# A gated layer computed by Strassen's scheme: product M6 ahead of M5 in the quads without a tile after M6, and five smaller moves

## The chip, the cores and the metric

The kernel runs on one core of one Trainium2 chip. The metric is the device time of one execution in microseconds (us), smaller is better. The times of the kernel before are 2017.08, 2018.61 and 2018.64 us, median 2018.61.

## What is computed

Three layers follow one another on 2304 tokens of 512 features. Attention over pooled keys and a mixture of eight experts come first; the change touches neither. The third layer is the one changed:

```python
g = x @ w_gate                           # 2304x512 by 512x1536
silu = g * (1.0 / (1.0 + np.exp(-g)))
val = x @ w_val
return (silu * val @ w_out).astype(np.float32)
```

## The kernel before

**Numbers.** Every fp32 product is made of three matmuls: both operands are split into a high and a low part, and high*high, high*low and low*high are summed in PSUM (`mm3`, L117 to L119).

**Quads.** Tokens go in three passes of 768. A matrix product of a token block with 256 columns of weights is done by Strassen's scheme: seven half-size products M1 to M7 of six matmuls each instead of eight. One such group is a *quad* (`quad`, L1130). M1, M6, M7 and M4 are summed one after the other in PSUM bank a (`aps`), M2 goes to bank b (`bps`), M5 and M3 to bank c (`cps`). The order written out is M1, M2, M5, M6, M7, M4, M3. After M1, M6 and M7 ScalarE copies the state of bank a to SBUF (`part_sum`, L1113: copies s1, u2, u3); the next product into bank a has to wait for that copy. VectorE then adds the copies to banks b and c (`whole`, L1199), which gives the four quarters "11", "22", "21", "12".

**Gate and value.** The gated layer takes a gate quad and a value quad in turn for each 256 of the 1536 columns (loop variable `m`, six per pass). A gate quad ends each quarter with a sigmoid on ScalarE (L1606) and a product on VectorE (L1607). A value quad multiplies its quarters by them (L1622 in pass 1, L1636 in passes 2 and 3). In pass 1 the result is split (L1626, L1627) and the second layer follows as six plain token tiles (`yps`, L1184 to L1186, added on VectorE at L1788), which `fill_y` puts after M6 and after M7 of the next two quads. In passes 2 and 3 the second layer is by Strassen too, over two values of `m`, so over four quads (x = 0 gate, 1 value, 2 gate, 3 value): `split_b` (L1355 to L1357), the sums `sum_t13` and `sum_t24` (L1361, L1365), the splits `split_t` (L1346 on ScalarE, L1348 on GpSimd), and seven *blocks* (`gated_block`, `mbs`, L1684 to L1686, 18 matmuls each), put after M7 of x = 0 and after M2 and M7 of x = 1, 2, 3. No block and no tile stands after M6. VectorE adds each block to SBUF (L1691). When a pass is complete, `finish` (L1666) adds the blocks to the output rows (L1659) and stores them.

**What sets the order.** The program's order on each engine is written by hand: each quad takes a table `tasks` of work to issue after each of its products, and a queue `late` of work that is issued one step later. An engine works strictly in that order. So the sigmoid of "11" (issued late, after M5) stands ahead of the copy u2 in ScalarE's queue.

**Weights of the output matrix.** In pass 1 each gate quad also prepares 256 rows of `w_out` for the later passes: two row splits (L65, L66), four row sums on VectorE (`take_row_sums`, L190), their split (`split_gated_sums`, L879 on ScalarE, L882 on GpSimd), and stores to DRAM (`store_rows`, `store_gated_sums`, L886). The split sets return in passes 2 and 3 through three slots of 512 KB (`gated_set`, `load_gated`, L1652).

Of the kernel before, what the change touches and what calls it, by code (L numbers as in the profile page):

```python
# [29 lines left out]
def fused_kernel(ctx: ExitStack, tc, q, k, v, w_gate, w1, w2, v_gate, v_val, v_out, out):  # L30
# [8 lines left out]
    P = 128  # L39
# [576 lines left out]
    with tc.manual_schedule():  # L616
# [173 lines left out]
        def load_rows(i):  # L790
            if i < NQ or NE <= i < NE + NG:
                if i < NE + 2:
# [77 lines left out]
        def gated_row_sums(i):  # L870
            for f in take_row_sums(nc.vector, rraw[i], part_of(10.5, 8 * P, F32).rearrange("p (m f) -> p m f", m=4)):
                f()
# [259 lines left out]
        def quad(i, ys, tasks, sink, back=0):  # L1132
# [28 lines left out]
            prod(c, "M5", True)  # L1161
            after("M5")
# [3 lines left out]
            fill_y(per - back)  # L1166
# [3 lines left out]
            fill_y(per)  # L1170
# [47 lines left out]
        def next_weights(i, n, tasks, first=False):  # L1218
# [13 lines left out]
            if n is not None:  # L1232
# [14 lines left out]
                if not expert:  # L1247
                    at("M5", lambda: gated_row_sums(n))
                    at("M4", split_gated_sums)
# [395 lines left out]

        def gated_set(v):
            return part_of(60.5 + 4 * (v % 3), 8 * P).rearrange("p (q h f) -> p q h f", q=2, h=2)
# [27 lines left out]
        def gated_block(v, at_once=False):  # L1675
# [11 lines left out]
            load_gated(v + 3)  # L1687
# [15 lines left out]
        def pair_tasks(m, x, tasks):  # L1703
# [11 lines left out]
            if x == 0 and j:  # L1715
                merge(tasks, {"M6": [lambda: split_t(1, "M6", "22", G)], "M4": [lambda: split_t(1, "M5", "11", G)]})
            if j == 0 and x == 3:
# [4 lines left out]
        for m in range(NPASS * SP2):  # L1722
# [9 lines left out]
            if m < 2:  # L1732
                if m:
                    merge(tasks, {"M1": [lambda: split_rows(NE, 0), lambda: split_rows(NE, 1)],
                                  "M2": [lambda: store_rows(NE), lambda: gated_row_sums(NE)],
                                  "M5": [lambda: load_rows(NE + 1)], "M4": [split_gated_sums]})
# [12 lines left out]
            quad(i, more, tasks, gate_sink(gs, m, g), 2 if m == 1 else 0)  # L1749
# [21 lines left out]
            quad(i + 1, more, tasks, pair_sink(gs, g) if p else value_sink(gs, hs, n))  # L1771
# [63 lines left out]
```

## Time and profile before

| what | value |
|---|---|
| device time, three runs | 2017.08, 2018.61, 2018.64 us |
| the profiled execution | 2015.87 us |
| its span, first to last instruction | 2014.0 us |
| TensorE (PE) busy | 1965.8 us, 98% |
| VectorE (DVE) busy | 1494.9 us, 74% |
| GpSimd (POOL) busy | 1391.4 us, 69% |
| ScalarE (ACT) busy | 909.8 us, 45% |
| mean granted TensorE clock | 0.998 |
| the gated layer in the span | about 1575 to 2014 us |
| its pass 1, pass 2, pass 3, the end | to 1700, to 1838, to 1988, to 2014 |

Busy times say which engine has the least room. PE has, so what can be gained is its idle time: the waits of PE, stretch by stretch, and the work on another engine that ends each of them. A matmul of 384 columns is listed with 0.34 us, but the next one starts 0.17 us after it, so products are measured from start to start.

### The profile page before, as it was taken

Reading aid. Unit: us, or ns where it says so; the run is one execution under the profiler, and the core shown is the slowest. Engines: PE = TensorE matmul, PEld = TensorE weight load, DVE = VectorE, ACT = ScalarE, POOL = GpSimd, SP = SyncE. Lnnn points to the kernel's source line nnn. Section 1 sums busy time; section 2 is a strip of 40 time slices with the busy share of each in tenths; the row PEclk is TensorE's granted clock in tenths of the full one; section 3 lists DMA queues with packets and bytes.
Section 4 is the critical chain, followed back from the end, with each engine's and each line's share of the span. In section 5 each row is a group of like instructions: output and inputs, shape, how many; then the busy total and the mean of one; then the engine's idle time right before and its main releaser. Section 6 shows DMA issues by size and latency. Waiting matters only on the chain.

```text
span 2014.0 us, 32218 instructions
## 1 busy us (share of the span) xinstructions
PE 1965.8 (98%) x11405; PEld 1881.1 (93%) x11405; DVE 1494.9 (74%) x2310; ACT 909.8 (45%) x1751; POOL 1391.4 (69%) x1260
## 2 busy tenths in 40 slices
PE   8999999999999999999999999999999999998998
PEld 7899899899999999999999999999999888898997
DVE  7764868777777778777877888777777877667766
ACT  4443434444444534443434434444445555555552
POOL 7674668887888367767677667776776777676554
PEclk9999999999999999999999999999999999999999
DMA  7674587888888898889898898899886664644544
GB/s 201 188 197 126 216 286 252 320 304 312 291 316 303 302 327 320 317 302 317 298 324 310 280 334 318 306 310 317 310 302 237 226 244 152 214 158 157 188 161 142
DMA packets 230223, 528.03 MB, mean 262 GB/s; under 512 B 36176, under 2 KB 116144, under 8 KB 226224
## 3 DMA queue, kind: packets, MB, share of 16 engines
q1 hardware_dynamic: 226896, 522.85, 75.1%
q0 software_dynamic: 3168, 3.15, 1.1%
q8 instruction: 90, 1.47, 0.3%
q14 instruction: 69, 0.57, 0.1%
HBM read 370.16 MB, written 155.76 MB: 261 GB/s over the span
## 4 chain that ended last, share of the span: by engine, by line
PE 88%; DVE 7%; ACT 2%; issue 2%; DMA 1%; POOL 0%; SPq 0%; DVEq 0%; ACTq 0%; POOLq 0%
PE aps L117 8%; PE aps L119 8%; PE aps L118 8%; PE mbs L117 7%; PE mbs L118 7%; PE mbs L119 7%; PE yps L1184 4%; PE yps L1186 4%; PE yps L1185 4%; PE cps L117 4%; PE cps L119 4%; PE cps L118 4%; PE bps L117 2%; PE bps L118 2%; PE bps L119 2%
## 5 line engine op out<-in xcount | busy, mean ns | idle before, releaser
L1348 POOL TENSOR_TENSOR LR<-LF,LR 128x384 fp32r<-128x384 f32 x288 | 314.7, 1116 | 185.1 <-ACT LR L1346 184.9
L1113 ACT COPY LF<-aps 128x384 f32<-128x384 f32 x378 | 181.6, 480 | 407.9 <-PE aps L119 406.1
L117 PE MATMUL mbs<-LR 128*128 128x384 f32 x840 | 283.1, 337 | 0.0
L118 PE MATMUL mbs<-LR 128*128 128x384 f32 x840 | 282.5, 336 | 0.0
L119 PE MATMUL mbs<-LR 128*128 128x384 f32 x840 | 281.9, 336 | 0.0
L1395 DVE TENSOR_TENSOR AC<-mbs,AC 128x768 f32<-128x768 f32 x196 | 187.1, 955 | 126.6 <-PE mbs L119 126.1
L851 POOL TENSOR_TENSOR LR<-praw,LR 128x512 fp32r<-128x512 f32 (+1 forms) x130 | 136.9, 1074 | 106.0 <-ACT LR L843 105.9
L851 POOL TENSOR_TENSOR LR<-sums,LR 128x512 fp32r<-128x512 f32 (+1 forms) x101 | 168.0, 1678 | 23.9 <-ACT LR L843 23.9
L1184 PE MATMUL yps<-LR 128*128 128x512 f32 x432 | 169.5, 392 | 0.5 <-DVE AC L1447 0.5
L1361 POOL TENSOR_TENSOR LF<-LF 128x384 f32<-128x384 f32 x120 | 129.8, 1082 | 57.2 <-DVE LF L1515 45.4
L1186 PE MATMUL yps<-LR 128*128 128x512 f32 x432 | 168.7, 391 | 0.0
L1185 PE MATMUL yps<-LR 128*128 128x512 f32 x432 | 168.3, 390 | 0.0
L1355 ACT COPY LF<-bps 128x384 f32<-128x384 f32 x144 | 69.3, 481 | 217.3 <-DVE bps L1515 183.7
L118 PEld LDWEIGHTS mbs<-LR 128*128 128x128 f32 x840 | 157.8, 188 | 0.0
L119 PEld LDWEIGHTS mbs<-LR 128*128 128x128 f32 x840 | 157.7, 188 | 0.0
L117 PEld LDWEIGHTS mbs<-LR 128*128 128x128 f32 x840 | 157.6, 188 | 0.0
L1346 ACT ACTIVATE LR<-LF 128x768 fp32r<-128x768 f32 x144 | 122.0, 848 | 48.9 <-PE mbs L119 43.2
L1449 DVE SCALAR_TENSOR_TENSOR AC<-yps,pr,AC 128x512 f32<-128x512 f32 x168 | 121.2, 744 | 30.8 <-PE yps L1186 27.0
L1365 POOL TENSOR_TENSOR LF<-LF 128x384 f32<-128x384 f32 x120 | 132.3, 1103 | 9.4
L1199 DVE TENSOR_TENSOR bps<-cps,LF 128x384 f32<-128x384 f32 x126 | 70.8, 562 | 74.8 <-ACT LF L1113 74.5
L66 POOL TENSOR_TENSOR LR<-LF,LR 128x1024 fp32r<-128x1024 f32 x24 | 60.3, 2512 | 69.2 <-ACT LR L65 63.9
L66 POOL TENSOR_TENSOR LR<-rraw,LR 128x512 fp32r<-128x512 f32 x64 | 88.5, 1405 | 28.3 <-ACT LR L65 23.9
(341 smaller groups left out, 6228.3 us busy)
## 6 DMA issues: line engine op xcount, KB each, us to landing
LR<-w1s_d SPq DMA_DIRECT2D x210, 512.0 KB
LR<-w2s_d SPq DMA_DIRECT2D x210, 512.0 KB
w1s_d<-LR SPq DMA_DIRECT2D x29, 1792.0 KB
w2s_d<-LR SPq DMA_DIRECT2D x24, 1024.0 KB
w2s_d<-LR SPq DMA_DIRECT2D x90, 256.0 KB
LR<-w3s_d SPq DMA_DIRECT2D x42, 512.0 KB
praw<-in_moe_w_dram SPq DMA_DIRECT2D x30, 512.0 KB
rraw<-in_moe_w_dram SPq DMA_DIRECT2D x30, 512.0 KB
```

The lines of the kernel that those rows point to most:

```text
L66: nc.gpsimd.tensor_tensor(out=lo, in0=src, in1=hi.bitcast(F32), op=ALU.subtract)
L117: nc.tensor.matmul(ps, lhsT=wh, rhs=ah, start=start, stop=False, skip_group_check=more)
L118: nc.tensor.matmul(ps, lhsT=wh, rhs=al, start=False, stop=False, skip_group_check=more)
L119: nc.tensor.matmul(ps, lhsT=wl, rhs=ah, start=False, stop=stop, skip_group_check=more)
L851: nc.gpsimd.tensor_tensor(out=lo[:, c], in0=src[:, c], in1=hi[:, c].bitcast(F32), op=ALU.subtract)
L1113: nc.scalar.copy(out=t, in_=ps[:, :HB])
L1184: nc.tensor.matmul(ps, lhsT=hh[:, o:o + P], rhs=wh, start=j == 0, stop=False)
L1185: nc.tensor.matmul(ps, lhsT=hh[:, o:o + P], rhs=wl, start=False, stop=False)
L1186: nc.tensor.matmul(ps, lhsT=hl[:, o:o + P], rhs=wh, start=False, stop=j == 1)
L1348: eng.tensor_tensor(out=lo[:, c], in0=src[:, c], in1=hi[:, c].bitcast(F32), op=ALU.subtract)
L1365: eng.tensor_tensor(out=r_of(q, a), in0=r_of(q, a), in1=r_of(q, b), op=ALU.subtract)
L1395: nc.vector.tensor_tensor(out=acc_of(m), in0=ps[:, :, :HB], in1=acc_of(m), op=ALU.add)
```

## The change

1. `quad` gets an argument `swap`: the order is then M1, M2, M6, M5, M7, M4, M3. It is set in all quads of passes 2 and 3 and in the gate quad of m = 1. Tiles that stood after M6 go after M7.
2. The four row sums L190, which were issued together after M5, are issued two after M4 and two after M3 of the gate quad (m = 1: of both quads). Their split moves into the value quad, after M1, and the store after M7. The raw rows of one `w_out` part get a place of their own.
3. At the start of pass 3 the sums `sum_t13` and `sum_t24` of the pass before are issued after M4 and M3 of x = 0 instead of M1 and M2, the splits after them in x = 1.
4. `finish` issues its seven additions in other places.
5. At the end, the first of the last seven blocks is issued between the two sums.
6. Three of the last four weight sets go to another, free region and are loaded in the last quad, the fourth when the first of the last seven blocks is done.

```diff
-        def quad(i, ys, tasks, sink, back=0):
+        def quad(i, ys, tasks, sink, back=0, swap=False):
...
             c = new_c()
-            prod(c, "M5", True)
-            after("M5")
+            if not swap:
+                prod(c, "M5", True)
+                after("M5")
             prod(a, "M6", False)
             u2 = part_sum(a, "u2")
             after("M6")
-            fill_y(per - back)
+            if swap:
+                prod(c, "M5", True)
+                after("M5")
+            else:
+                fill_y(per - back)
             prod(a, "M7", False)
             u3 = part_sum(a, "u3")
             after("M7", ("22", c, u3))
-            fill_y(per)
+            fill_y(len(ys) - back if swap else per)
...
         def gated_row_sums(i):
-            for f in take_row_sums(nc.vector, rraw[i], part_of(10.5, 8 * P, F32).rearrange("p (m f) -> p m f", m=4)):
-                f()
+            t = part_of(10.5, 8 * P, F32).rearrange("p (m f) -> p m f", m=4)
+            steps = deque()
+
+            def two():
+                if not steps:
+                    steps.extend(take_row_sums(nc.vector, rraw[i], t))
+                for _ in range(2):
+                    steps.popleft()()
+
+            return {"M4": [two], "M3": [two]}
...
         def finish(p, m, other):
             V = nc.vector
-            return {"M1": [add_of(V, "M2", "M1"), add_of(V, "M6", "M1")],
-                    "M2": [out_rows(p, "M2", 0, 0)],
-                    "M6": [add_of(V, "M7", "M6"), add_of(other, "M3", "M6")],
-                    "M5": [add_of(other, "M3", "M5"), out_rows(p, "M3", 0, 1)],
+            return {"M2": [add_of(V, "M2", "M1"), out_rows(p, "M2", 0, 0)],
+                    "M6": [add_of(V, "M6", "M1"), add_of(other, "M3", "M6")],
+                    "M5": [add_of(V, "M7", "M6"), add_of(other, "M3", "M5"), out_rows(p, "M3", 0, 1)],
...
+            change = j > 0 and j % NGP == 0
             if x in (0, 2) and (x or j):
                 q = 0 if x else 1
-                merge(tasks, {"M1": [lambda: sum_t13(q, V)], "M2": [lambda: sum_t24(q, V)]})
+                m1, m2 = ("M4", "M3") if change and x == 0 else ("M1", "M2")
+                merge(tasks, {m1: [lambda: sum_t13(q, V)], m2: [lambda: sum_t24(q, V)]})
...
+            if x == 3 and 7 * (j + 1) == len(GORDER):
+                merge(tasks, {"M1": [lambda v=v: load_gated(v) for v in range(LAST, LAST + 3)]})
...
                 if m == 2:
-                    merge(tasks, {"M1": [lambda: store_gated_sums(NE + 1)]})
+                    merge(tasks, {"M5": [split_gated_sums], "M7": [lambda: store_gated_sums(NE + 1)]})
+                merge(tasks, gated_row_sums(n))
...
             elif 1 < m < SP2:
-                merge(tasks, {"M5": [lambda: store_gated_sums(n)]})
+                merge(tasks, {"M1": [split_gated_sums], "M7": [lambda: store_gated_sums(n)]})
...
+        while side:
+            side.popleft()()
+        v = len(GORDER) - 7
         sum_t13(1, nc.vector)
+        gated_block(v, True)
         sum_t24(1, nc.vector)
         split_t(1, "M6", "22", nc.gpsimd)
         split_t(1, "M5", "11", nc.gpsimd)
-        while side:
-            side.popleft()()
-        for k in range(7):
-            gated_block(len(GORDER) - 7 + k, True)
+        for k in range(1, 7):
+            gated_block(v + k, True)
```

Line numbers grow by 10 to 30 in the changed kernel. The pieces below show what stands on two engines' queues, first before, then after the change.

ScalarE at x = 0 of a regular pair in pass 2: a split L1346 of the quad ahead (L1358 after the change), copies of bank a (L1113; L1123), the sigmoid of "11" (L1606 from bank b; L1618), the weight split (L843; L845).

```order
L1346 ACTIVATE LR<-LF 128x2x384
L1113 COPY LF<-aps 128x384
L1606 ACTIVATE LF<-bps 128x384
L1113 COPY LF<-aps 128x384
L843 ACTIVATE LR<-praw_17380 128x2x256
L843 ACTIVATE LR<-praw_17380 128x256
```

```order
L1358 ACTIVATE LR<-LF 128x2x384
L1123 COPY LF<-aps 128x384 x2
L1618 ACTIVATE LF<-bps 128x384
L845 ACTIVATE LR<-praw_17379 128x2x256
L845 ACTIVATE LR<-praw_17379 128x256
```

The copies s1 and u2 now follow each other, and the sigmoid of "11" stands behind u2.

VectorE from the gate quad of m = 2 into its value quad: the sigmoid products (L1607; L1619), tile additions (L1788; L1812), additions of a copy to a bank (L1199; L1214), the row sums (L190 in both), the value products (L1622; L1634).

```order
L190 TENSOR_TENSOR LF<-AC 128x256
L190 TENSOR_TENSOR LF<-AC,LF 128x256
L1607 TENSOR_TENSOR LF<-bps,LF 128x384
L1788 TENSOR_TENSOR AC<-yps,AC 128x512 x2
L1199 TENSOR_TENSOR bps<-cps,LF 128x384
L1788 TENSOR_TENSOR AC<-yps,AC 128x512
L1607 TENSOR_TENSOR LF<-bps,LF 128x384
L1607 TENSOR_TENSOR LF<-aps,LF 128x384
L1199 TENSOR_TENSOR cps<-cps,LF 128x384
L1607 TENSOR_TENSOR LF<-cps,LF 128x384
L1199 TENSOR_TENSOR bps<-bps,LF 128x384
L1622 TENSOR_TENSOR bps<-bps,LF 128x384
```

```order
L1214 TENSOR_TENSOR bps<-cps,LF 128x384
L1812 TENSOR_TENSOR AC<-yps,AC 128x512
L1619 TENSOR_TENSOR LF<-bps,LF 128x384
L190 TENSOR_TENSOR LF<-AC 128x256
L190 TENSOR_TENSOR LF<-LF,AC 128x256
L1619 TENSOR_TENSOR LF<-aps,LF 128x384
L1214 TENSOR_TENSOR cps<-cps,LF 128x384
L190 TENSOR_TENSOR LF<-AC 128x256
L190 TENSOR_TENSOR LF<-AC,LF 128x256
L1619 TENSOR_TENSOR LF<-cps,LF 128x384
L1214 TENSOR_TENSOR bps<-bps,LF 128x384
L1634 TENSOR_TENSOR bps<-bps,LF 128x384
```

Before, all four sums (two of them are the first rows of the piece) stand ahead of the addition for "22" (bps<-cps); after, two stand ahead of the addition for "12" (cps<-cps) and two ahead of the one for the next quad's "11" (bps<-bps).

VectorE at the end of the program: sums `sum_t13` and `sum_t24` (L1361, L1365; L1373, L1377), the blocks' additions (L1691; L1708), the additions of `finish` (L1659; L1674).

```order
L1361 TENSOR_TENSOR LF<-LF 128x384 x2
L1365 TENSOR_TENSOR LF<-LF 128x384 x2
L1691 TENSOR_TENSOR AC<-mbs,AC 128x768
L1659 TENSOR_TENSOR AC<-AC 128x768 x2
L1691 TENSOR_TENSOR AC<-mbs,AC 128x768 x3
L1659 TENSOR_TENSOR AC<-AC 128x768
L1691 TENSOR_TENSOR AC<-mbs,AC 128x768 x2
L1659 TENSOR_TENSOR AC<-AC 128x768
L1691 TENSOR_TENSOR AC<-mbs,AC 128x768
```

```order
L1373 TENSOR_TENSOR LF<-LF 128x384 x2
L1708 TENSOR_TENSOR AC<-mbs,AC 128x768
L1377 TENSOR_TENSOR LF<-LF 128x384 x2
L1708 TENSOR_TENSOR AC<-mbs,AC 128x768 x2
L1674 TENSOR_TENSOR AC<-AC 128x768
L1708 TENSOR_TENSOR AC<-mbs,AC 128x768
L1674 TENSOR_TENSOR AC<-AC 128x768
L1708 TENSOR_TENSOR AC<-mbs,AC 128x768
L1674 TENSOR_TENSOR AC<-AC 128x768
L1708 TENSOR_TENSOR AC<-mbs,AC 128x768
L1674 TENSOR_TENSOR AC<-AC 128x768
L1708 TENSOR_TENSOR AC<-mbs,AC 128x768
```

The first block's addition now stands between the sums, and the two additions of `finish` behind it are gone from there.

## Rows read from the trace of the kernel before

**Rows 1.** the page, busy time, share of the span and instructions of each engine

```profile
PE 1965.8 (98%) x11405; PEld 1881.1 (93%) x11405; DVE 1494.9 (74%) x2310; ACT 909.8 (45%) x1751; POOL 1391.4 (69%) x1260
```

**Rows 2.** stretches: length, busy (count) PE PEld DVE ACT POOL, clock, DMA, GB/s

```profile
1838.00:1860.00 22.00, 17.65 (x100) 16.50 (x99) 19.34 (x27) 12.62 (x24) 16.99 (x13) 0.92 0.40 142
...
1988.00:2014.00 26.00, 17.91 (x131) 17.32 (x130) 17.00 (x20) 3.18 (x5) 16.91 (x11) 0.90 0.48 159
```

**Rows 3.** PE's waits (total, times, longest): 1575:1700, 1700:1743, 1743:1838, 1860:1988, 1988:2014

```profile
PE cps L117 <- DVE bps L1199: 4.9, 4, 2.1
PE aps L117 <- ACT LF L1113: 0.6, 1, 0.6
...
PE aps L117 <- ACT LF L1113: 2.1, 3, 0.8
PE cps L117 <- DVE bps L1199: 0.2, 1, 0.2
...
PE aps L117 <- ACT LF L1113: 5.5, 8, 1.2
...
PE aps L117 <- ACT LF L1113: 6.9, 11, 0.8
...
PE mbs L1684 <- DVE AC L1691: 1.9, 1, 1.9
PE mbs L1684 <- DMA LR<-w3s_d: 0.6, 1, 0.6
```

**Rows 4.** timeline, one quad of pass 2: start, us, engine, instruction, [idle <-releaser]

```profile
1757.39 0.34 PE L117 MATMUL cps<-T1h,LR 128*128 128x384 f32 x1
...
1758.43 0.34 PE L117 MATMUL aps<-T2h,LR 128*128 128x384 f32 x1
...
1759.30 0.34 PE L119 MATMUL aps<-T2h,LR 128*128 128x384 f32 x1
...
1759.67 0.48 ACT L1113 COPY LF<-aps 128x384 f32<-128x384 f32 x1 [1.76 <-PE aps L119]
...
1760.20 0.45 PE L117 MATMUL aps<-T3h,LR 128*128 128x384 f32 x1 [0.57 <-ACT LF L1113]
...
1761.36 0.28 PE L1684 MATMUL mbs<-LR 128*128 128x256 f32 x1
```

**Rows 5.** timeline, regular x = 0: copy s1, first matmul after M2

```profile
1792.05 0.48 ACT L1113 COPY LF<-aps 128x384 f32<-128x384 f32 x1
...
1792.58 0.34 PE L117 MATMUL cps<-T1h,LR 128*128 128x384 f32 x1
```

**Rows 6.** timeline, pass 2's first gate quad: the same two

```profile
1703.98 0.34 PE L117 MATMUL cps<-T1h,LR 128*128 128x384 f32 x1
...
1704.04 0.47 ACT L1113 COPY LF<-aps 128x384 f32<-128x384 f32 x1
```

**Rows 7.** timeline of pass 3's first gate quad, PE and ScalarE

```profile
1841.74 0.42 PE L117 MATMUL cps<-T1h,LR 128*128 128x384 f32 x1 [1.04 <-DVE LF L1636]
...
1842.18 0.50 ACT L1113 COPY LF<-aps 128x384 f32<-128x384 f32 x1
...
1846.24 0.49 ACT L1606 ACTIVATE LF<-bps 128x384 f32<-128x384 f32 x1 [2.82 <-DVE bps L1199]
...
1847.16 0.44 PE L117 MATMUL aps<-T3h,LR 128*128 128x384 f32 x1 [3.08 <-ACT LF L1113]
```

**Rows 8.** sums L190: whole kernel (ns min/median/max), stretch 1575:1700 (busy)

```profile
L190 DVE TENSOR_TENSOR LF<-rraw x52: 412/950/1512, 304.9 to 1601.3; 128x256 f32<-128x256 f32 x52
...
1575.00:1700.00 125.00, 31.04 (x24) 0.00 (x0) 1.00 0.64 219
```

**Rows 9.** timeline of the end, GpSimd and VectorE

```profile
1995.15 5.34 POOL L1348 TENSOR_TENSOR LR<-LF,LR 128x384 fp32r<-128x384 f32 x4 [2.02 <-ACT LR L1346]
...
2002.20 7.02 POOL L1659 TENSOR_TENSOR AC<-AC 128x768 f32<-128x768 f32 x3 [1.71 <-DVE AC L1691]
...
2008.49 0.96 DVE L1691 TENSOR_TENSOR AC<-mbs,AC 128x768 f32<-128x768 f32 x1 [0.96 <-PE mbs L1686]
```

More of the change, by code (lines that the diff above doesn't have):

```diff
@@ L791, in load_rows @@
             if i < NQ or NE <= i < NE + NG:
-                if i < NE + 2:
+                if i == NE + 1:
+                    rraw[i] = part_of(88.5, 8 * P).bitcast(F32).rearrange("p (j d) -> p j d", j=2)
+                elif i < NE + 1:
                     rraw[i] = rawp.tile([P, 2, DM], F32, tag="raw", name=f"rraw{i}")
@@ L1246, in next_weights @@
                 at("M3", lambda: store_rows(n))
-                if not expert:
-                    at("M5", lambda: gated_row_sums(n))
-                    at("M4", split_gated_sums)
             at("M5", lambda: pair_sums(i + 1))
@@ L1644, in fused_kernel @@
         GORDER = [(j, m) for j in range((NPASS - 1) * NGP) for m in GX]
+        LAST = len(GORDER) - 4
         def gated_set(v):
-            return part_of(60.5 + 4 * (v % 3), 8 * P).rearrange("p (q h f) -> p q h f", q=2, h=2)
+            at = 32.5 + 4 * (v - LAST) if LAST <= v < LAST + 3 else 60.5 + 4 * ((v - 6 if v > LAST else v) % 3)
+            return part_of(at, 8 * P).rearrange("p (q h f) -> p q h f", q=2, h=2)
         def load_gated(v):
@@ L1686, in gated_block @@
                     nc.tensor.matmul(y, lhsT=hl, rhs=w[:, q, 0], start=False, stop=q == 1)
-            load_gated(v + 3)
+            if v + 3 < LAST:
+                load_gated(v + 3)
+            elif v == LAST - 3:
+                load_gated(LAST + 3)
             if j % NGP == 0:
@@ L1709, in pair_tasks @@
             V, G = nc.vector, nc.gpsimd
+            change = j > 0 and j % NGP == 0
             if x in (0, 2) and (x or j):
                 q = 0 if x else 1
-                merge(tasks, {"M1": [lambda: sum_t13(q, V)], "M2": [lambda: sum_t24(q, V)]})
+                m1, m2 = ("M4", "M3") if change and x == 0 else ("M1", "M2")
+                merge(tasks, {m1: [lambda: sum_t13(q, V)], m2: [lambda: sum_t24(q, V)]})
             if x == 3:
                 merge(tasks, {"M4": [lambda: split_t(0, "M6", "22", G)], "M3": [lambda: split_t(0, "M5", "11", G)]})
-            if x == 0 and j:
+            if x == 1 and change:
+                merge(tasks, {"M2": [lambda: split_t(1, "M6", "22", G)], "M5": [lambda: split_t(1, "M5", "11", G)]})
+            if x == 0 and j and not change:
                 merge(tasks, {"M6": [lambda: split_t(1, "M6", "22", G)], "M4": [lambda: split_t(1, "M5", "11", G)]})
+            if x == 3 and 7 * (j + 1) == len(GORDER):
+                merge(tasks, {"M1": [lambda v=v: load_gated(v) for v in range(LAST, LAST + 3)]})
             if j == 0 and x == 3:
@@ L1734, in fused_kernel @@
                     merge(tasks, {"M1": [lambda: split_rows(NE, 0), lambda: split_rows(NE, 1)],
-                                  "M2": [lambda: store_rows(NE), lambda: gated_row_sums(NE)],
-                                  "M5": [lambda: load_rows(NE + 1)], "M4": [split_gated_sums]})
+                                  "M2": [lambda: store_rows(NE)], "M5": [lambda: load_rows(NE + 1)]})
+                    merge(tasks, gated_row_sums(NE))
                 next_weights(i, None, tasks)
@@ L1748, in fused_kernel @@
                 merge(tasks, {"M2": [lambda n=("T1", "T3")[l - 3]: sum_x(n, nc.gpsimd)]})
-            quad(i, more, tasks, gate_sink(gs, m, g), 2 if m == 1 else 0)
+            quad(i, more, tasks, gate_sink(gs, m, g), 2 if m == 1 else 0, p > 0 or m == 1)
             tasks = last_blocks(1) if m == 0 else {}
@@ L1755, in fused_kernel @@
                 merge(tasks, {"M1": [lambda: split_rows(NE + 1, 0)], "M2": [lambda: split_rows(NE + 1, 1)],
-                              "M5": [lambda: store_rows(NE + 1), lambda: store_gated_sums(NE), lambda: gated_row_sums(NE + 1)],
-                              "M4": [split_gated_sums]})
+                              "M5": [lambda: store_rows(NE + 1), split_gated_sums], "M7": [lambda: store_gated_sums(NE)]})
+                merge(tasks, gated_row_sums(NE + 1))
             elif 1 < m < SP2:
-                merge(tasks, {"M5": [lambda: store_gated_sums(n)]})
+                merge(tasks, {"M1": [split_gated_sums], "M7": [lambda: store_gated_sums(n)]})
             if l == SP2 - 1 and p + 1 < NPASS:
@@ L1770, in fused_kernel @@
                 more = deque(ys.popleft() for _ in range(min(2, len(ys))))
-            quad(i + 1, more, tasks, pair_sink(gs, g) if p else value_sink(gs, hs, n))
+            quad(i + 1, more, tasks, pair_sink(gs, g) if p else value_sink(gs, hs, n), 0, p > 0)
             if m == SP2 + 1:
```

## The prediction

> **What bounds the kernel now.** I read the busy line first: PE is busy for 1965.8 of 2014.0 us and the next engine, DVE, for 1494.9 [rows 1]. The change adds and removes no PE work, so it can only gain PE's idle time, 48 us in all, and only in the gated layer, from 1575 us on. Second I read PE's waits there, stretch by stretch [rows 3]. In the steady parts of passes 2 and 3 one wait counts: bank a waits for ScalarE's copy L1113, 8 times (5.5 us) and 11 times (6.9 us). In pass 1 bank c waits four times (4.9 us) for DVE's L1199. At the end a block waits 1.9 us for DVE and one 0.6 us for its weights. Third, the timeline of each place, to see what ends the wait. Fourth, the granted clock: 0.92 in the stretch around the start of pass 3 and 0.90 at the end, where it is 1.2 instead of 2.4 GHz for a while [rows 2].
>
> **What a wait costs.** In the quad of [rows 4] M5 takes 1.04 us from its first matmul to M6's (1757.39 to 1758.43). M6 takes 1.77 to M7 (1760.20), and M7 takes 1.16 to the block (1761.36). So the quad loses 0.73 + 0.12 = 0.85 us where the listed idle time is 0.57. I therefore price each wait at its listed time plus 0.28.
>
> **Passes 2 and 3, regular quads.** There are 24 quads, and 18 of them lie in the steady parts: all of the 8 + 11 waits but the longest of pass 2 (1.15, listed as 1.2), which I count below. Their idle time is 5.5 - 1.15 + 6.9 = 11.25 us, their cost 11.25 + 18 x 0.28 = 16.3 us. With M5 between M6 and M7 the copy has more time. From M6's last matmul to M7 it needs 0.90 us now (1759.30 to 1760.20), and 0.24 us more in the worst of the 18 (idle 0.8 [rows 3]). M5 gives 1.04 + 0.17 = 1.21. So both fit, the second with 0.06 to spare. The sigmoid of "11", which stood ahead of the copy at x = 0, now stands behind it. What is late next: M6 now follows M2 without M5 between, and reads bank a after copy s1. Where a block follows M2 (x = 1, 2, 3) that has 2 us in hand. At x = 0 it has not: s1 ends at 1792.05 + 0.48 = 1792.53, M2's end leaves PE free at 1792.58 [rows 5]. It just fits. I take 16.3; the bounds are 16.3 and, if s1 or u2 is late by one ScalarE instruction (0.5) in half of them, 9 x (0.5 + 0.28) = 7 less: 9.3.
>
> **Start of pass 2.** The waits are 2.1 us in 3 and 0.2 in one [rows 3], and the 1.15 left over above: 3.45 + 5 x 0.28 = 4.9 us. Of these the wait of M4 in the one quad without block or tile after M7 stays (2.1 / 3 + 0.28 = 1.0), and so does the 0.2 + 0.28, at the end of pass 1's last value quad. New is a wait of M6 for s1: in the first gate quad s1 ends at 1704.51, M2 at 1703.98 [rows 6]; with 0.05 until PE starts and 0.12 to restart that is 0.7 us. I take the same once more for the next x = 0, where the pair behind it has no block. Gain: 4.9 - 1.0 - 0.5 - 1.4 = 2.0; bounds 0 and 3.4.
>
> **Start of pass 3.** Now M5 waits 1.04 and M7 waits 3.08 us [rows 7]. The second is a chain: the sums on DVE, behind them L1199 for "11", behind that the sigmoid (1846.24), behind that copy u2, then M7. After it the clock was low. A granted clock of 0.92 over 22 us is at most (1 - 0.92) x 22 = 1.8 us. Together 1.32 + 3.36 + 1.8 = 6.5. The change takes the sums and the sigmoid out of that chain. But s1 itself is late: it starts at 1842.18 and ends at 1842.68, because ScalarE works off the splits for the new pass, while M2 ended 1.20 us before M5's start at 1841.74, at 1840.54. Nothing in the change shortens that queue; M5 stood there before and hid it in part, and now M6 stands there. So M6 waits 2.2 to 2.6 us. The copy u3 one quad earlier meets the same queue, about 0.9. Listed stalls of 3.08 and 1.9 us were followed by the low clock [rows 2, 3], the one of 2.1 us in pass 1 was not (1.00 in [rows 8]), so I charge half of 1.8. Gain: 6.5 - 2.6 - 0.9 - 0.9 = 2.1; bounds -1 and 5.5.
>
> **Pass 1.** The waits are 4.9 + 0.6 us in five, so 5.5 + 1.4 = 6.9 us. The four sums of a gate quad take 31.04 / 6 = 5.2 us of DVE [rows 8]. Moved behind M4 and M3, they no longer stand ahead of "22", for which M3 waits. They stand ahead of the next quad's "11" instead. Count from M4's end: 0.5 + 2.6 (two sums) + 0.5 + 0.6 + 2.6 + 0.5 + 0.6 + 0.6 = 8.5 us until the value product of "11", then 0.5 for its split and 0.5 for u2 on ScalarE: 9.5. M7 is due after five products and two tiles, 5.2 + 2.7 = 7.9. That would be 1.6 + 0.28 in each of the value quads of m = 2, 3, 4, more than the wait that goes. With sums at their shortest, 0.41 us, it would be 6 us and no wait. The split L879 stands ahead of u2 there too (1.06 us), and in m = 5 it meets the splits for pass 2, about 1 us. I take a middle: 4.4 us come back, gain 2.5; bounds -5 and 6.9.
>
> **A rule on the sums.** L190 takes 0.41 us at its shortest, 1.5 at its longest [rows 8]. The Trainium skill, page "SBUF — State Buffer", section "SBUF: two separate sides", says why this could be: a VectorE instruction with two SBUF inputs and a GpSimd instruction that reads SBUF exclude each other from a shared pair of ports for the whole instruction. The trace agrees in size; by that rule the cost of the move hangs on whether GpSimd works then, and with an idle GpSimd pass 1 would gain 6.9. GpSimd has its sums' split L851 after M4 and waits for L879 later, so the second pair of sums may be the cheap one.
>
> **The end.** DVE's last block addition starts at 2008.49; GpSimd's last addition ends at 2002.20 + 7.02 = 2009.22 [rows 9]. The block between the sums frees its bank two us sooner, and the weights are there, so most of 1.9 + 0.6 + 0.56 goes, and with it the low clock, (1 - 0.90) x 26 = 2.6 us at most. Two things take its place. The splits on ScalarE and GpSimd (1995.15, 5.34 for four) start about 0.9 later, since one addition now stands ahead of the second sum; block M6 and block M5 wait for them, about 1.6 us. And GpSimd's three additions (2.34 each, one behind the other) start only when those splits and one more DVE addition are done, near 2001.1, and end near 2008.1. Then GpSimd, not DVE, is last. Gain: 2009.45 - 2008.1 = 1.4; bounds 0 and 4. For loads that are sooner I cost nothing: they go to a region that the last quad no longer reads, on a queue with room (DMA share 0.48 [rows 2]).
>
> **Sum.** 16.3 + 2.0 + 2.1 + 2.5 + 1.4 = 24.3 us. The profiled execution took 2015.87 us, 1.87 over its span, so 1991.6 after. It lies 2.7 under the median of the three runs, 2018.61; against that median the forecast is 1994.3.
>
> **Rivals.**
> 1. *The waits come back elsewhere.* s1 and u2 stand close behind each other now, and ScalarE's queue is what PE waits for in any order. For it: 0.05 and 0.06 us of slack above, and pass 1's count of 9.5 against 7.9. Against it: ScalarE idles for 1.76 us ahead of the copy in the regular quad [rows 4]. Regular quads 9.3, pass 1 -3, the starts 2, the end 1: gain about 9, time 2009. Chance 0.18, with a gain from 4 to 17.
> 2. *All hides.* The sums run beside an idle GpSimd (6.9), the start of pass 3 reaches its bound (5.5), the end 4, the rest as above 18.3: gain 35, time 1984. Against it: s1's lateness there is in rows. Chance 0.08, with a gain over 31.
> 3. *Slower.* The sums of pass 1 lie wholly in PE's path: 6 x 5.2 = 31 us against the 24.3 + 4.4 that the rest is worth, so 2 us slower, 2021. It decides only if over 4.8 us of each group lie in front of a copy that M7 waits for. Against it: two tiles (2.7 us) stand between. Chance 0.03.
> 4. *The order is not what PE waits for.* If the copy were late for another reason than its place, M5 would only move the wait to itself. [Rows 4] speak against it: the copy starts right after M6's last matmul. Time 2018, chance 0.03.
>
> My forecast has 0.68, its own range 1988 to 2001. With rival 2 in part and most of rival 1 the range is 1986 to 2005. What a measurement here can tell from no change is 0.2%, 4 us. Faster by more: 0.68 + 0.08 + 0.18 = 0.94; within: 0.03; slower: 0.03.
>
> **What would show it.** In the profile after: the waits of bank a for L1113 in the steady stretches are gone (under 1 us of the 12.4); M6 waits for L1113 at the first gate quad of passes 2 and 3, over 2 us in the second; in pass 1 M7 in value quads waits for L1113 where M3 waited for L1199; at the end the last instruction before the stores is GpSimd's L1659 of before. Wrong would be: waits of M7 that stay; a wait of M6 at x = 0 in every pair; or DVE last at the end.

## The result, and the profile after

The changed kernel took 1990.43 us in the median of four runs (1989.64 to 1992.20), the kernel before 2018.62: a ratio of 0.9863, 95% interval 0.9846 to 0.9880, so 1.4% or 28 us faster. Against the median 1994.3 was forecast. The profiled execution took 1992.20 us with a span of 1990.2; 1991.6 was forecast for it. Between the two profiled spans lie 23.8 us. The other 4 us are a matter of which executions were profiled: the one of the kernel before (2015.87 us) was faster than all that were timed, the one of the changed kernel the slowest of its four.

PE's waits, in the same columns as [rows 3] (total, times, longest): first the stretch 1575:1700, then 1700:1743 (start of pass 2), 1743:1824 (rest of pass 2), three rows of 1824:1878 (start of pass 3), and 1959:1991 (the end). In 1878:1959 there is none.

```profile
PE cps L117 <- DVE bps L1214: 1.0, 1, 1.0
...
PE aps L117 <- ACT LF L1123: 1.8, 3, 0.7
...
PE aps L117 <- ACT LF L1123: 1.1, 2, 0.8
...
PE aps L117 <- ACT LF L1123: 2.5, 2, 1.3
PE bps L117 <- DVE LF L1619: 0.9, 1, 0.9
PE cps L117 <- DVE bps L1214: 0.6, 1, 0.6
...
PE mbs L1700 <- POOL LR L1360: 0.2, 1, 0.2
```

Of the regular quads' 18 waits for a copy one is left, M7's in pass 3's second quad (1.27 us), and one is new, M4's 0.81 us in pass 2; bank b's wait in pass 3's fourth quad grew from 0.5 to 0.9. No wait is longer than 1.3 us. The length of a quad, from its M1 to the next M1, says what each place gave (us; the last two columns are gains):

| place | before | after | gain | forecast |
|---|---|---|---|---|
| pass 1, nine quads from the gate quad of m = 1 | 110.1 | 103.2 | 6.9 | 2.5 |
| start of pass 2, six quads from m = 5's value quad | 63.1 | 64.2 | -1.1 | 2.0 |
| rest of pass 2, seven quads | 85.3 | 80.1 | 5.2 | 16.3 with the two below |
| first gate quad of pass 3 | 15.6 | 11.8 | 3.7 | 2.1 |
| the next ten quads | 122.2 | 115.3 | 6.9 | |
| last quad (0.85 of the gain), then to the last matmul | 31.9 | 27.7 | 4.2 | |
| last matmul to the end of the span | 5.9 | 7.6 | -1.8 | the end: 1.4 |

A regular quad after (timeline of PE and ScalarE, pass 2; compare [rows 4]):

```profile
1798.11 0.34 PE L119 MATMUL aps<-T2h,LR 128*128 128x384 f32 x1
1798.28 0.34 PE L117 MATMUL cps<-T1h,LR 128*128 128x384 f32 x1
...
1798.48 0.48 ACT L1123 COPY LF<-aps 128x384 f32<-128x384 f32 x1 [0.72 <-PE aps L119]
...
1799.32 0.34 PE L117 MATMUL aps<-T3h,LR 128*128 128x384 f32 x1
...
1800.36 0.28 PE L1698 MATMUL mbs<-LR 128*128 128x256 f32 x1
```

Copy u2 starts 0.37 us after M6's last matmul, as before, but M5 now fills the 1.04 us until M7; nothing waits. These quads went from 12.43 or 12.48 to 11.59 us.

Pass 3's first gate quad (compare [rows 7]):

```profile
1830.68 0.49 ACT L1123 COPY LF<-aps 128x384 f32<-128x384 f32 x1
...
1831.23 0.45 PE L117 MATMUL aps<-T2h,LR 128*128 128x384 f32 x1 [1.22 <-ACT LF L1123]
...
1838.46 0.44 PE L117 MATMUL cps<-LR 128*128 128x384 f32 x1 [0.63 <-DVE bps L1214]
```

M6 waits for s1, as forecast, but 1.22 us and not 2.2 to 2.6; M3 waits 0.63 us for VectorE, which was not forecast. The 3.08 us of M7 are gone, and the granted clock of 1824:1846 is 1.00 where [rows 2] had 0.92.

### The profile page after: what moved, and what is told of

Same layout as the page of the kernel before. It is cut to its first block, busy times and chain, and to the rows that moved or that the text cites. A ratio compares the mean times of both kernels' runs of the same rounds, so it can differ in the third digit from the quotient of the medians.

```text
span 1990.2 us, 32201 instructions
## 1 busy us (share of the span) xinstructions
PE 1958.1 (98%) x11405; PEld 1878.9 (94%) x11405; DVE 1478.7 (74%) x2310; ACT 910.0 (46%) x1751; POOL 1389.3 (70%) x1260
## 5 line engine op out<-in xcount | busy, mean ns | idle before, releaser
L1123 ACT COPY LF<-aps 128x384 f32<-128x384 f32 x378 | 181.4, 480 | 410.0 <-PE aps L119 401.2
L1373 POOL TENSOR_TENSOR LF<-LF 128x384 f32<-128x384 f32 x120 | 129.7, 1081 | 57.6 <-DVE LF L1527 45.9
L1199 PE MATMUL yps<-LR 128*128 128x512 f32 x432 | 169.4, 392 | 0.2 <-DVE AC L1459 0.2
L1358 ACT ACTIVATE LR<-LF 128x768 fp32r<-128x768 f32 x144 | 122.0, 848 | 50.8 <-PE mbs L119 43.5
L1377 POOL TENSOR_TENSOR LF<-LF 128x384 f32<-128x384 f32 x120 | 130.5, 1088 | 9.4
L1214 DVE TENSOR_TENSOR bps<-cps,LF 128x384 f32<-128x384 f32 x126 | 70.9, 563 | 71.0 <-ACT LF L1123 70.8
```

The costliest lines, as they stand in the source:

```text
L1123: nc.scalar.copy(out=t, in_=ps[:, :HB])
L1199: nc.tensor.matmul(ps, lhsT=hh[:, o:o + P], rhs=wh, start=j == 0, stop=False)
L1377: eng.tensor_tensor(out=r_of(q, a), in0=r_of(q, a), in1=r_of(q, b), op=ALU.subtract)
```

## The experiments

Each was timed against the kernel before on its own chip, so ratios, not times, compare across them. Runs 1 to 4 shared one chip, 5 to 8 a second (two executions each), 9 to 11 a third, and 12 ran on a fourth; the changed kernel itself is on record for its first timing and for run 1. What a move is worth is therefore read from the lengths of quads.

**1. The changed kernel again.** No edit.

> The changed kernel once more, to be compared with the others on one chip and to see how far one execution differs from another. Theory (the gain is as large as the traces of the gated layer show, 24 us from 1575 us on): ratio 0.986 to 0.988, and the stretches of the gated layer repeat within 0.3 us. Rival (part of the 28 us between the medians lies outside the gated layer and belongs to the executions): the span up to 1575 us differs by 1 us or more between executions.

1992.18 us, ratio 0.9871 [0.9857, 0.9886]. The quads repeat within 0.03 us, but for two at the start of pass 3 (11.94 and 12.16, 12.89 and 12.32), so the theory holds but for these. The rival holds in part: the gated layer started 0.9 us later than in the first profile, so about 1 us of a difference between two profiles lies outside the change.

**2. The new order alone.** The kernel before, with `quad` and its calls as in the change, nothing else.

> The kernel before with the new order M6, M5 alone. Theory (the order hides the copy u2, the rest of the change gives the rest): 12 us from the regular quads, 3 to 4 at the start of pass 3 since the sigmoid now stands behind the copy, 1 in the gate quad of m = 1; the waits of M3 in pass 1 (4.9 us) and those of the end stay: 16 to 18 us faster than before. Rival (the sums are what PE waits for): 8 us faster, with the wait of 3 us at the start of pass 3 still there.

1999.41 us, ratio 0.9909 [0.9894, 0.9923]: 18.8 us of the 26.1 that the whole change gains on this chip. That is a little over the 16 to 18 of the theory, and its terms differ. Of the 18 regular quads 17 gain 0.7 us or more; x = 0 in pass 2 gains nothing (10.62, before 10.61). Pass 1 gains nothing (110.3 us, before 110.1): m = 2's gate quad loses its wait, but M3's wait in m = 1 grows from 2.13 to 2.99 us, and the clock falls behind it; from m = 3 on M3's waits stay (12.55 a quad). Pass 3's first gate quad stays at 15.50, where the theory had 3 to 4 us: the wait moved from M7 to M4, as the timeline shows (VectorE, ScalarE, PE; L1366 are sums, L1204 the addition for "11", L1611 the sigmoid):

```profile
1838.90 2.66 DVE L1366 TENSOR_TENSOR LF<-LF 128x384 f32<-128x384 f32 x2
1841.48 0.55 DVE L1204 TENSOR_TENSOR bps<-bps,LF 128x384 f32<-128x384 f32 x1
...
1842.07 0.49 ACT L1611 ACTIVATE LF<-bps 128x384 f32<-128x384 f32 x1 [3.26 <-DVE bps L1204]
...
1844.75 0.47 ACT L1113 COPY LF<-aps 128x384 f32<-128x384 f32 x1
...
1845.27 0.44 PE L117 MATMUL aps<-LR 128*128 128x384 f32 x1 [2.79 <-ACT LF L1113]
```

The sums still delay "11", its sigmoid waits 3.26 us at the head of ScalarE's queue, and the next copy behind it is now u3 instead of u2. The three quads after it, however, fall from 38.9 to 34.8 us.

**3. All but the order.**

```diff
-quad(i, more, tasks, gate_sink(gs, m, g), 2 if m == 1 else 0, p > 0 or m == 1)
+quad(i, more, tasks, gate_sink(gs, m, g), 2 if m == 1 else 0)
```

(and the same for the value quad)

> The changed kernel with the old order M5, M6 in all quads, the rest of the change kept. Theory: the 18 regular waits come back with 0.85 us each, so 16 us, and with those of pass 2's start 16 to 19 us slower than the changed kernel (about 2008). Rival (sums are what PE waits for): 8 us slower or less.

2006.03 us, ratio 0.9942 [0.9927, 0.9957]: a gain of 12.2 us; the time is 13.9 us above run 1, a little less than the 16 to 19 of the theory. The regular quads are back at 12.4 to 12.5, but pass 3's first gate quad takes 11.41. So the new order gave the regular quads, and nothing to that one. 18.8 and 12.2 are 5.0 more than the 26.1 together. Most of it lies in pass 3's second to fourth quads, where the order alone does better: 38.9 us before, 34.8 in run 2, 38.3 in run 3, 38.0 in the changed kernel. Over pass 3's first four quads this makes 54.5 us before, 50.3 with the order alone, 49.7 without it and 49.8 with all of the change: what the changed kernel saves against run 2 in the first of them (3.7 us), it mostly loses again in the next three (3.1).

**4. The four row sums together again.**

```diff
-            return {"M4": [two], "M3": [two]}
+            return {"M5": [four]}
```

> The changed kernel with the four row sums of a gate quad together after M5 again, the rest of the change kept. Theory (spread sums run while GpSimd is idle and nothing waits behind them): the M3 waits of pass 1 for the addition L1214 come back, 1.1 us in each of m = 2, 3, 4, and up to 2.4 in m = 1: 4 to 6 us slower than the changed kernel. Rival of the forecast (a wait goes and another of the same size comes in the value quads): within 1.5 us of the changed kernel.

2004.67 us, ratio 0.9940 [0.9923, 0.9956]: 12.5 us slower than run 1, where I had counted 4 to 6. Pass 1's nine quads take 115.9 us, more than the 110.1 of the kernel before, so this is not wholly the old place: there the sums of m = 1's gate quad stood after M2, not after M5 as the list of the change has it. PE's waits in 1575:1700, and two windows of it (columns as in [rows 2]):

```profile
PE cps L117 <- DVE bps L1210: 8.2, 5, 2.6
```

```profile
1595.00:1600.00 5.00, 5.00 (x21) 5.00 (x22) 2.44 (x5) 2.87 (x7) 0.00 (x0) 0.66 0.68 214
1610.00:1615.00 5.00, 4.37 (x17) 4.37 (x18) 4.05 (x8) 2.29 (x6) 0.56 (x1) 0.71 0.87 287
```

8.2 us of waits, 5 x 0.28 to restart, and 1.7 + 1.5 us of low clock behind the two of 2.5 make 12.8. Spreading the sums is what pass 1 gained by: without it no gain is left, the order alone (run 2) has none, and run 3, which has the spread sums in the old order, takes 103.7 us there.

**5. The sums beside a busy GpSimd.** Two extra GpSimd additions, which read SBUF, are put ahead of each pair of sums.

```diff
-            return {"M4": [two], "M3": [two]}
+            return {"M4": [busy, two], "M3": [busy, two]}
```

> The changed kernel with two idle additions of 256 columns (from constants, into a buffer nobody reads) on GpSimd ahead of each pair of row sums, 24 of them in all; nothing else changes. They add GpSimd time only. Theory (a sum is short because GpSimd is idle then): the sums L190 take 1 us or more on average in pass 1 instead of about 0.7, VectorE falls behind, and the M7 of value quads waits for the copy as forecast, 1 us or more in each: 3 to 8 us slower. Rival (the place in the order matters, not what GpSimd does): the sums take longer but no PE wait over 0.3 us appears in pass 1; within 1 us.

1992.80 us, ratio 0.9886 [0.9857, 0.9915]. The sums L190 in 1610:1690 (ns, min/median/max), first of the changed kernel, then of this one:

```profile
L190 DVE TENSOR_TENSOR LF<-AC x8: 409/630/705, 1614.0 to 1685.6; 128x256 f32<-128x256 f32 x8
L190 DVE TENSOR_TENSOR LF<-LF,AC x4: 1346/1346/1348, 1614.8 to 1683.4; 128x256 f32<-128x256 f32 x4
L190 DVE TENSOR_TENSOR LF<-AC,LF x4: 412/412/415, 1617.5 to 1685.9; 128x256 f32<-128x256 f32 x4
```

```profile
L190 DVE TENSOR_TENSOR LF<-AC x8: 593/718/850, 1615.8 to 1687.4; 128x256 f32<-128x256 f32 x8
L190 DVE TENSOR_TENSOR LF<-LF,AC x4: 1344/1346/1347, 1616.7 to 1685.2; 128x256 f32<-128x256 f32 x4
L190 DVE TENSOR_TENSOR LF<-AC,LF x4: 958/959/960, 1619.4 to 1688.1; 128x256 f32<-128x256 f32 x4
```

The last sum of a quad takes 0.96 instead of 0.41 us. All 24 sums (columns as in [rows 8]; changed kernel, then this one):

```profile
1575.00:1700.00 125.00, 16.33 (x24) 0.00 (x0) 1.00 0.69 224
```

```profile
1575.00:1700.00 125.00, 22.29 (x24) 0.00 (x0) 1.00 0.67 222
```

That is 2.7 us for a group of four and 3.7 here, after 5.2 before. Even so no M7 waits in the value quads of m = 2, 3 and 4: so half of the theory fell. Half of the rival fell too: m = 2's gate quad grows from 11.41 to 13.25 us, with a wait of M7 of 0.90, and in m = 5's value quad M7 waits 0.47. So 1 us more on each group costs some 1.8 us in all of pass 1's nine quads, and the sums in one place (run 4) 12.7. How much of the 1.8 comes from GpSimd's own delay the run does not show.

**6. The sums of the pass before, and the splits after them, in their old place.**

```diff
-            change = j > 0 and j % NGP == 0
+            change = False
```

> The changed kernel with the sums and splits at the start of pass 3 at their old places (after M1 and M2, splits in the same quad). Theory (the 3.08 us wait went because the sigmoid stands behind the copy u2 now): the wait of M7 does not come back; the split L1358 stands ahead of the copy u3, so M4 waits 0.5 to 1 us: 0 to 1.5 us slower in that quad. Rival (the sums' place ended it): the first quad of pass 3 takes 3 us or more longer, and the granted clock falls to 0.5 behind it.

1993.53 us, ratio 0.9889 [0.9861, 0.9918]; pass 3's first gate quad is 15.80 us again. The theory fell: the place of these sums, not the order of M5 and M6, ended the wait there. Over the first four quads 52.7 us stand against 49.8. M4's first matmul, and the window behind it:

```profile
1837.88 0.69 PE L117 MATMUL aps<-LR 128*128 128x384 f32 x1 [2.80 <-ACT LF L1123]
```

```profile
1837.90:1843.80 5.90, 5.90 (x18) 5.90 (x19) 3.53 (x6) 2.60 (x4) 5.90 (x6) 0.50 0.24 99
```

It is the wait of run 2, and for 5.9 us after it the granted clock is 0.50, 1.2 GHz.

**7. The last weight sets loaded as before.** Three slots for all sets, `load_gated(v + 3)` after each block.

> The changed kernel with the weight sets of the last four blocks in the three old slots, each loaded when a block frees one. Theory (at the end GpSimd's three additions are last, so the load has room): the last block waits up to 0.8 us for its weights, and the span from the last M3 to the end grows by 0 to 0.5 us. Rival (the loads were what the end waited for): 1 us or more longer.

1989.58 us, ratio 0.9870 [0.9841, 0.9898]; the end is unchanged within 0.1 us (27.83 and 7.52, together 35.35 against 35.31). The sooner loads gave nothing: no wait for weights is left either way. Its span of 1988.1 is 2.1 below the changed kernel's by other things, which no edit made; 1.9 of it lie in the two quads that follow. PE's wait at the start of pass 2:

```profile
1696.82 0.44 PE L119 MATMUL aps<-B11h,LR 128*128 128x384 f32 x1 [0.93 <-POOL LR L853]
```

The profiles of runs 6, 7 and 9 have this wait in M1 of pass 2's first gate quad, and m = 5's value quad and that quad take 23.1 us together; in the changed kernel and runs 1, 8, 10, 11 and 12 M3, M6 and M7 wait there one after the other, and it is 25.0 (run 3, in the old order: 25.2). Up to there all of these but run 3 issue the same work as the changed kernel. Which pattern comes goes with a meeting of VectorE and GpSimd in m = 5's value quad. The changed kernel, then run 7:

```profile
1691.85 1.31 POOL L853 TENSOR_TENSOR LR<-sums,LR 128x512 fp32r<-128x512 f32 x1
1691.95 2.03 DVE L733 TENSOR_TENSOR B21l<-xq,B21h 128x768 fp32r<-128x768 f32 x1 [2.14 <-ACT B21h L732]
```

```profile
1692.15 0.96 DVE L733 TENSOR_TENSOR B21l<-xq,B21h 128x768 fp32r<-128x768 f32 x1 [1.95 <-ACT B21h L732]
1692.22 2.06 POOL L853 TENSOR_TENSOR LR<-sums,LR 128x512 fp32r<-128x512 f32 x1
```

When GpSimd starts first, VectorE's split takes 1.9 to 2.1 us, and the addition that M3 waits for comes late (the changed kernel, runs 1, 3, 8, 10, 11 and 12); when VectorE starts first, it takes 0.96 (runs 6, 7 and 9). The two starts lie 0.02 to 0.22 us apart in all ten profiles. No run sets their order on purpose, so this is seen, not tested.

**8. The first of the last blocks behind both sums again.**

```diff
         sum_t13(1, nc.vector)
-        gated_block(v, True)
         sum_t24(1, nc.vector)
```

> The changed kernel with the first of the last seven blocks behind both sums again, the additions at their new places. Theory: PE waits about 1.9 us for VectorE's first addition again, and the clock may fall behind it; GpSimd's splits start 0.9 us sooner than in the changed kernel; the span from the last M3 to the end grows by 0 to 1.5 us. Rival (the block's place gave the whole gain of the end): 2.5 us or more longer.

1995.13 us, ratio 0.9897 [0.9869, 0.9926]. The end takes 30.22 instead of 27.69. A block's first matmul and the window from it:

```profile
1973.58 0.41 PE L1698 MATMUL mbs<-LR 128*128 128x256 f32 x1 [1.91 <-DVE AC L1708]
```

```profile
1973.58:1977.19 3.61, 3.61 (x17) 3.61 (x18) 0.81 (x1) 0.75 (x2) 3.52 (x4) 0.53 0.00 0
```

The 1.91 us wait of [rows 3] is back, and the low clock with it. From the last quad's M1 to the end of the span it is 37.8 us instead of 35.3, 2.4 more: close to the rival's 2.5, and not the 0 to 1.5 of the theory.

**9. Splits behind the copies.** What the change left, first: ScalarE and PE at x = 0 in pass 2 of the changed kernel.

```profile
1789.54 0.84 ACT L1358 ACTIVATE LR<-LF 128x768 fp32r<-128x768 f32 x1 [1.19 <-DVE LF L1377]
1790.29 0.46 ACT L1123 COPY LF<-aps 128x384 f32<-128x384 f32 x1
...
1790.80 0.44 PE L117 MATMUL aps<-LR 128*128 128x384 f32 x1 [0.81 <-ACT LF L1123]
```

The split waits for the sum L1377, the copy u3 behind it for nothing but the split.

```diff
-merge(tasks, {"M6": [... split_t(1, "M6", "22", G)], "M4": [... split_t(1, "M5", "11", G)]})
+merge(tasks, {"M4": [... split_t(1, "M6", "22", G)], "M3": [... split_t(1, "M5", "11", G)]})
```

(at the change of pass: x = 1, from M2 and M5 to M5 and M7)

> The changed kernel, with only the splits of T4 and T1 (M6/22 and M5/11 of the pair before) moved on ScalarE: at x = 0 from behind M6 and M4 to behind M4 and M3, and in the first pair of pass 3 from x = 1's M2 and M5 to its M5 and M7. Theory: in the changed kernel these splits wait for VectorE's sums and hold up the copy behind them, so PE waits before M4 at x = 0 in pass 2 (0.25 and 0.81 us) and before M7 in pass 3's second quad (1.27 us). Behind the copies they hold up nothing: the x = 0 quads of pass 2 go from 10.97 to about 10.5 (its wait for s1 stays) and from 10.63 to about 9.6, pass 3's second quad from 13.13 to about 11.6; gain 3 us, about 1987.5. Rival: the splits are then late for the blocks of x = 2 that read them, or hold up the next quad's s1 and sigmoids; gain under 1 us, about 1990.

1991.12 us, ratio 0.9872 [0.9855, 0.9888]. The x = 0 quads: 10.97 to 9.95 and 10.63 to 9.54, and their waits of M4 are gone, as the theory had it. Of the first one's 1.02 us only some 0.4 belong to the edit: in runs 4, 5, 7, 8 and 10 this quad takes 10.4 without it, since M6's wait for s1 there is 0.25 to 0.27 us in them and 0.69 in the changed kernel. Pass 3's second quad: only 13.13 to 12.41, and the third grew from 11.94 to 12.75. That half fell. The time cannot be told apart from the changed kernel's.

**10. `finish`'s additions at the change of pass as before the change** (two behind block M1, one behind M6); at the end as changed.

> The changed kernel, with the additions of finish at the change from pass 2 to pass 3 in their old places (two behind block M1, one behind M6); at the end of the program they stay in the new places. Theory: the new places put two or three of them in a row on VectorE in x = 2 and x = 3 of pass 3's first two pairs, ahead of a sigmoid product that frees bank b, and PE waits 0.88 us there; with the old places these quads go from 11.94 and 12.89 to 11.6 each: gain 1.6 us, about 1989. Rival: the additions behind block M1 then stand in the first two quads, where VectorE is late already, and these (11.84 and 13.13) grow by as much: no gain, 1990 to 1991.

1993.01 us, ratio 0.9877 [0.9863, 0.9892]. The third and fourth quads fell to 11.58 and 11.59, and the second grew from 13.13 to 14.98: the rival's case, nothing gained.

**11. Both moves.**

> The changed kernel with both moves: the splits behind the copies, and the additions of finish at the change of pass in their old places. Theory: the two waits have separate causes, the gains add: 3 + 1.6, about 1986. Rival: in pass 3's first quads both hang on one queue, VectorE's, so that taking one away lets the other wait grow: gain of 2 to 3, about 1988.

1990.84 us, ratio 0.9868 [0.9853, 0.9883]. The x = 0 quads keep their gain; pass 3's first four quads take 50.6 us, after 49.8 in the changed kernel, 49.9 in run 9 and 50.0 in run 10. Moving work within VectorE's queue moves the wait and leaves the sum: the rival in direction, but even its 2 us are not there.

**12. Work taken off VectorE.** The splits at x = 0 as in run 9, and three of `finish`'s additions at the change of pass on GpSimd.

```diff
-                steps = finish(1 + j // NGP, m, nc.gpsimd if at_once else nc.vector)
+                steps = finish(1 + j // NGP, m, nc.gpsimd)
```

> The changed kernel, with two moves: the splits at x = 0 stand behind M4 and M3, as in the run before that moved them (but in pass 3's second quad they stay in x = 1's M2 and M5), and at the change to pass 3 the three of finish's seven additions that GpSimd does at the end are GpSimd's there too. Theory: what remains lost in pass 3's first four quads (49.8 us, where 46 to 47 would be free of waits) is VectorE's load: it is busy for 45 of the 49.8 us, and moving work about inside its queue left the sum at 49.8 to 50.6. Three additions of 1 to 2 us fewer on it: the third and fourth quads go from 11.94 and 12.89 to about 11.6 each, the four to about 48.3; with 2.1 us of the x = 0 quads about 3.6 us in all, a profiled span near 1986.5 and a time near 1988. Rival: an addition takes GpSimd 2.3 us and shuts VectorE out of its way as long, and GpSimd's weight splits come later by up to 7 us, so PE waits for them in the third to fifth quads: 50 or more for the four, time 1990 or more.

1989.14 us (1988.93 to 1990.89), ratio 0.9864 [0.9847, 0.9880]. The four quads take 48.2 us, the third and fourth 11.58 and 11.68. Both kernels over these four quads (length, busy PE, PEld, DVE, ACT, POOL, clock), the changed one first:

```profile
1827.77:1877.57 49.80, 45.71 (x296) 43.95 (x296) 45.21 (x61) 27.10 (x53) 33.72 (x26) 1.00 0.57 182
```

```profile
1825.61:1873.83 48.22, 45.12 (x295) 44.03 (x295) 41.62 (x58) 27.29 (x53) 37.51 (x29) 1.00 0.55 178
```

VectorE is 3.6 us less busy, GpSimd 3.8 more, and the stretch is 1.6 shorter. Within these four quads only the engine of three additions differs, so VectorE's load is what kept the third and fourth long; the second stays at 13.11. The rival shows in the fifth quad, which grows from 9.84 to 10.31: there the copy u3 stands behind a weight split that waits for its transfer.

```profile
1880.59 0.94 ACT L845 ACTIVATE LR<-praw 128x512 fp32r<-128x512 f32 x2 [1.78 <-DMA praw<-val_d]
1881.44 0.46 ACT L1123 COPY LF<-aps 128x384 f32<-128x384 f32 x1
...
1881.95 0.44 PE L117 MATMUL aps<-LR 128*128 128x384 f32 x1 [0.50 <-ACT LF L1123]
```

By the quads from m = 1 on this version is 3.1 us ahead of the changed kernel; its time (ratio 0.9864 against 0.9863 and 0.9871) does not tell them apart. No run takes back by itself the split of the row sums in the value quad or the new places of `finish`'s additions at the end; what these two are worth stays open.

## Why the prediction was right, and which terms were not

The sum was 24.3 us; 23.8 came between the profiled spans and 28 between the medians. What was right is the main mechanism: 18 quads that waited for a copy, and M5 as the work that hides it. That the sum came out so close is partly luck: pass 1 gave 4.4 more than its term and the start of pass 3 1.6 more, the start of pass 2 3.1 and the regular quads 3.4 less. The premise that only PE's idle time can be gained does not quite hold: PE's busy time fell too, from 1965.8 [rows 1] to 1958.1 us, with 11405 matmuls in both. The restart behind a wait and the matmuls at the low clock are listed as busy.

**Regular quads (16.3, measured 12.9).** The mechanism and the price of a quad (0.85) were right; runs 2 and 3 show that the order alone does it. Of 18 quads 13 came down to the length without a wait (11.59; x = 0: 9.54). At x = 0 I checked the slack of s1, which held, and of u2, and not that of u3, the third copy: behind the new order a split that waits for VectorE stands ahead of it (run 9). Three quads of pass 3 that I counted as regular lie where VectorE is full and gained 0.07 to 0.54; two of them came free in run 12. So the sign that these waits are gone, with under 1 us left, did not come: it is 0.81 and 1.27 us, and the second is a wait of M7 that stayed and grew from 0.57.

**Pass 1 (2.5, measured 6.9).** I charged 4.4 us for sums in front of u2, from a count of 9.5 us against 7.9. No M7 of a value quad of m = 2, 3 and 4 waited for it. In m = 3 M4 of the gate quad ends at 1636.68, the copy u2 is the first of these rows, and M7 is not held up:

```profile
1642.64 0.47 ACT L1123 COPY LF<-aps 128x384 f32<-128x384 f32 x1
...
1644.61 0.34 PE L117 MATMUL aps<-T3h,LR 128*128 128x384 f32 x1
```

So it is 6.4 us against 7.9. What was wrong is the price of the sums: a group takes 2.7 us in the new place, the third and fourth 0.41 each with GpSimd idle (in m = 5 for 3.10 us), where it took 5.2. That is the side that the prediction named and did not take. The Trainium skill, "SBUF — State Buffer", section "SBUF: two separate sides", has a VectorE instruction with two SBUF inputs and a GpSimd instruction that reads SBUF exclude each other for the whole of the one that starts first, and run 5 agrees (0.41 to 0.96 us). With 2.5 us less the count is 7.0, so its other terms were some 0.6 too long. At the old price u2 would have come about 1 us after M7 was due (6.4 + 2.5 = 8.9, an estimate); no run reached that, for in run 5, with 3.7 us a group, u2 ends at 7.4.

**Start of pass 2 (2.0, measured -1.1).** The wait of M6 for s1 is there (0.40, forecast 0.7). Not forecast were 0.40 on the operand T2l and 0.52 of M7 there, and the wait of M3 ahead of them, 0.96 where 0.2 was. They come with the pattern in which VectorE's split L733 is late (run 7), so the sign of this term is not the change's alone: with the short pattern the six quads take 62.2 (run 6) or 61.7 us (run 7), a gain of 0.9 or 1.5. The split of the row sums, which meets the splits for pass 2 in m = 5's value quad, I had put at 1 us under pass 1; that it makes the two engines meet is likely, but no run takes it away alone. The new order alone keeps these two quads at 23.0, all the rest without it makes 25.2 of them.

**Start of pass 3 (2.1, measured 3.7).** The sign and the place of M6's wait were right. The sentence that nothing shortens ScalarE's queue for s1 was wrong: s1 starts 0.8 us after M2's end, not 1.64 as in [rows 7]. The order does it: s1 starts 2.91 us after the quad's M1 in the changed kernel and in runs 2 and 6, 3.51 in run 3 and 3.71 before. The 0.9 us for u3 one quad earlier did not come (that quad takes 11.59), and M3's 0.63 us did. And I gave the gain to the order of M5 and M6 and to the sums together; for this quad runs 2, 3 and 6 give it to the sums alone. Over the first four quads it is less plain: taking the sums' place back costs 2.9 us (run 6), but the order alone gets to 50.3 us without it, against 49.8 in the changed kernel. The clock did not fall, so its whole charge came back, not half.

**The end (1.4, measured 1.6).** Right in the sum and in the last engine: GpSimd, as the timeline of GpSimd and VectorE shows beside [rows 9]. The 1.6 us that block M6 and block M5 should wait for the splits are 0.23. The forecast's own rows give GpSimd's start as 1995.15 + 0.9 + 5.34 = 2001.4, not 2001.1, and a gain of 1.0.

```profile
1978.52 6.86 POOL L1674 TENSOR_TENSOR AC<-AC 128x768 f32<-128x768 f32 x3 [0.90 <-DVE AC L1674]
...
1983.82 0.96 DVE L1708 TENSOR_TENSOR AC<-mbs,AC 128x768 f32<-128x768 f32 x1
```

GpSimd ends at 1985.38, VectorE at 1984.78. The block between the sums is worth 2.4 us (run 8), the loads nothing (run 7); so the rest of the change costs some 0.8 at the end (2.4 less 1.6).

**The rivals.** None took place. Rival 1's mechanism shows at x = 0 in pass 2 and in pass 3's second quad, rival 2's in pass 1. Of the signs that would have been wrong, M6 waits at x = 0 in three quads of six, not in every pair, and VectorE is not last at the end.

## What to carry to other kernels

When an order is changed so that one copy gets time, count the slack of every copy on that engine's queue, and look for an instruction ahead of it that itself waits for a third engine: it passes the wait on. Where shifting a piece of work moves a wait and leaves the stretch's length, that engine's load is the first suspect: run 12, which took work off it, shortened the stretch where runs 9 to 11 did not. And a forecast whose sum is right can have its terms wrong by 3 to 4 us each way; compare stretch by stretch.

## What the runs showed of the hardware

The granted clock fell to 0.50 (1.2 GHz) after PE's waits of 1.91 us (run 8 and the kernel before), 2.5 (run 4, twice), 2.80 (run 6), 2.79 and 2.99 (run 2) and 3.08 (the kernel before). It stayed at 1.00 after 1.27 (changed kernel) and 1.75 (run 10), after the 2.13 of pass 1 in the kernel before, and at the end of run 2:

```profile
1979.01 0.39 PE L1689 MATMUL mbs<-LR 128*128 128x256 f32 x1 [1.92 <-DVE AC L1696]
```

```profile
1978.00:1986.00 8.00, 5.85 (x46) 5.65 (x47) 6.30 (x7) 1.58 (x2) 5.34 (x4) 1.00 0.60 183
```

So the length of a wait alone does not tell whether the clock falls. Where it fell, it cost 1.7 us beyond the wait in run 8 ((1 - 0.53) x 3.61) and about 3 in run 6 (half of 5.90).

Second, VectorE and GpSimd hold each other up by a microsecond, and which of them starts first decides which is held up: in the rows shown with run 7 the same two splits, in m = 5's value quad, take 2.03 and 1.31 us, or 0.96 and 2.06, with starts 0.1 us apart. That quad and the next then take 25.0 or 23.1 us together. This seems to change from one execution to the next: of run 9's four executions the profiled one, with the short pattern, took 1989.38 us and the others 1991.04 to 1991.55. In the short pattern ScalarE's weight split L845, ahead of them, starts 5.34 to 5.37 us after the quad's M1, in the long one 5.46 to 5.65; why stays open.
